# Two edits in the first batch of an attention and feed-forward kernel: how K and Q are loaded, and which engine forms one scaled V

## The chip, the cores and the metric

The kernel runs on one core of a Trainium2 chip. The core has a matrix engine (TensorE, PE in the profile, with its weight loads as PEld), three engines for element-wise work (VectorE, DVE; ScalarE, ACT; GpSimd, POOL) and a sync engine (SyncE, SP), each with its own stream of instructions in program order. Transfers between HBM and the on-chip memory (SBUF) are issued by SP, ACT or POOL and run on 16 DMA engines. TensorE writes to PSUM, from which VectorE and ScalarE read. The metric is the device time of one execution in microseconds (us); before the change it is 201.16 us, the median of three runs (200.54 to 201.26).

## The reference, cut to what matters

```python
# q, k, v: (4 batches, 8 heads, 768 positions, 64), float32
scores = q @ k.transpose(0, 1, 3, 2) / sqrt(64)
causal = rel >= 0                                   # rel = query position - key position
stream = causal & (pos[None, :] < 4 | (rel < 64))   # first 4 keys, or a window of 64
mask   = where(is_retrieval[head], causal, stream)
a      = softmax(where(mask, scores, -1e9))
x      = (a @ v), heads side by side                # (3072, 512)
h      = max(x @ w1, x @ w2, x @ w3)                # (3072, 768)
out    = h @ w_out                                  # (3072, 512)
```

A head is either a retrieval head (causal) or a streaming head. For blocks of keys far from the query, a streaming head keeps only the first four keys. The kernel does this with a second copy of V: `va` holds V, with a column of ones beside it for the sum, and `vf` holds V times a factor per head (`far`), which is 1 for a retrieval head and for the first four keys, and 0 elsewhere.

## The kernel before

The first batch is loaded in pairs of heads, each in two halves of 384 positions. K goes through SP's queue and Q through ACT's. With `alone`, a load of two pairs is issued as one transfer for each pair; without it, as one transfer for both.

```python
def load_pairs(half, hp, n, engines, alone=False):
    for nm, src, eng in zip(("ks", "qs"), (k, q), engines):
        st = stage.tile([P, 4, HB, D], FP32, tag=nm, name=nm)
        m = 2 if alone else 2 * n
        for h in range(0, 2 * n, m):
            eng.dma_start(out=st[:, h : h + m], in_=src[...])
        for i in range(n):
            staged.setdefault((half, hp + i), []).append(st[:, 2 * i : 2 * i + 2])
...
load_pairs(0, 0, 1, (nc.sync, nc.scalar))
ir32 = consts.tile([1, 2 * H], mybir.dt.int32, name="ir32")
nc.sync.dma_start(out=ir32, in_=is_retrieval...)
load_pairs(0, 1, 1, (nc.sync, nc.scalar))
load_pairs(0, 2, 2, (nc.sync, nc.scalar), True)
load_v(0, 0)                       # three transfers on SP, one for each block of 128 positions
```

Each pair is then cast to 16 bits (`cast_pair`: `kn`, `qn`), turned by TensorE (`turn_pair`, into `KQ`), and used for the scores. What is issued on each engine stands in this order:

```python
cast_pair(0, 0, (act, act))
...
cast_pair(0, 1, (pool, act))
turn_pair(0, 1, dve)
cast_pair(0, 2, (pool, pool))
scores(0, 0, (0,))
scores(0, 1, (0,))
...
load_weight(0)                     # w0t, issued by GpSimd
scores(0, 0, (1,))
far_flags()                        # VectorE writes far, GpSimd copies it into vf
cast_pair(0, 3, (pool, pool))
...
turn_pair(0, 2, dve)
scores(0, 1, (1,))
turn_pair(0, 3, dve)
...
load_pairs(1, 0, 2, (nc.gpsimd, nc.gpsimd))
...
load_weight(1)
...
load_pairs(1, 2, 2, (nc.gpsimd, nc.gpsimd))
load_weight(2)
load_v(0, 1, (nc.gpsimd,) * HB)
...
load_weight(3)
```

After this start the kernel follows a list of slots. In each, some scores are computed, with units of the feed-forward network (`ffn`) between them, and four short lists of other work are issued. `prep_v` forms `va` and `vf` for one pair of heads; its two letters name the engine of the copy and that of the product.

```python
def prep_v(t, i, op, vf_engine):
    ...
    op(out=vdst, in_=vs[:, hs])                       # va
    vf_engine.tensor_tensor(                          # vf = va * far, 128 x 384 in half 1
        out=vf[j][:, hs, k0:k1, 0:D],
        in0=vs[:, hs, 0:1] if half == 0 else va[j][:, hs, k0:k1, 0:D],
        in1=far[:, hs, k0:k1].unsqueeze(3).to_broadcast([P, 2, k1 - k0, D]),
        op=ALU.mult,
    )
...
PROGRAM = (
    (2.4, True, "", "", "cast 1 2 dp", ""),
    (2.4, False, "load 1 0", "", "cast 1 3 da", ""),
    (2.0, False, "", "pair 1 2", "load 1 1", ""),
    (2.2, False, "pair 1 3", "v 2 0 ap", "", "v 2 1 ap"),
    (2.2, False, "", "gate, load_v 1 0", "", ""),
    (1.6, True, "", "av 2 0", "", "turn 1 0 0 0"),
    ...
```

The network accumulates in PSUM, in a pool of four banks that also serves the turned tiles and the products with V. VectorE frees a bank when it takes the maximum over the three weights:

```python
for wi, ni in order:                                  # first batch: all of w1, then w2, then w3
    yy = psum()
    ... four matmuls with w_t[wi] ...
    if wi == 0:
        nc.scalar.copy(out=acc[ni], in_=yy[:, 0:HALF])
    else:
        dst = acc[ni] if wi == 1 else hT[ni]
        nc.vector.tensor_tensor(out=dst, in0=yy[:, 0:HALF], in1=acc[ni], op=ALU.max)
```

Of the kernel before, what the change touches and what calls it, by code (L numbers as in the profile page):

```python
# [51 lines left out]
def kernel(  # L52
# [14 lines left out]
    nc = tc.nc  # L67
# [53 lines left out]
# [5 lines that stand above are left out]
                eng.dma_start(  # L126
                    out=st[:, h : h + m],
                    in_=src[
                        0, 2 * hp + h : 2 * hp + h + m, half * HALF : (half + 1) * HALF
                    ].rearrange("h (p j) d -> p h j d", p=P),  # L130
                )
            for i in range(n):
                staged.setdefault((half, hp + i), []).append(st[:, 2 * i : 2 * i + 2])
# [13 lines left out]
    def turn_pair(half, hp, *engines):  # L147
        if (0, hp // 2) not in KQs:
            KQs[0, hp // 2] = qkt.tile([P, 2, S, 2], FP16, tag="KQ", name="KQ")
        xs = cast.pop((half, hp))  # L150
        n = 2 // len(engines)
        for part, op in enumerate(engines):
            tr = bank([P, 1024], FP16, "tr")
            for i in range(n):
                for j in range(HB):
                    c = i * HALF + j * P
                    nc.tensor.transpose(  # L157
                        tr[:, c : c + P],
                        xs[part + i][:, j].rearrange("p h d -> p (h d)"),
                        ident,  # L160
                    )
            op(
                out=of_pair(hp)[
                    :, part : part + n, half * HALF : (half + 1) * HALF
                ].rearrange("p i (t j) -> p i t j", j=HB),
                in_=tr[:, 0 : n * HALF].rearrange("p (i j t) -> p i t j", i=n, j=HB),
            )
# [35 lines left out]
    def load_v(b, half, engines=None):  # L203
        engines = engines or (nc.sync,) * HB
        vs = stage.tile([P, H, HB, D], FP32, tag="vs", name="vs")
        for j in range(HB):
            r0 = half * HALF + j * P
            engines[j].dma_start(
                out=vs[:, :, j], in_=v[b, :, r0 : r0 + P].rearrange("h p d -> p h d")
            )  # L210
        staged_v[b, half] = vs
# [2 lines left out]
    ir32 = consts.tile([1, 2 * H], mybir.dt.int32, name="ir32")  # L214
    nc.sync.dma_start(out=ir32, in_=is_retrieval.bitcast(mybir.dt.int32).unsqueeze(0))
    load_pairs(0, 1, 1, (nc.sync, nc.scalar))
    load_pairs(0, 2, 2, (nc.sync, nc.scalar), True)
    load_v(0, 0)


# [165 lines left out]
    def prep_v(t, i, op, vf_engine):  # L386
        b, half, qd = where(t)
        vs = staged_v[b, half]
        j, k0 = b % 2, half * HB
        hs = slice(4 * qd + 2 * i, 4 * qd + 2 * i + 2)  # L390
        vdst = va[j][:, hs, k0 : k0 + HB, 0:D]
        op(out=vdst, in_=vs[:, hs])  # L392
        k0, k1 = ((0, 1), (1, 4))[half]
        vf_engine.tensor_tensor(  # L394
# [5 lines that stand above are left out]
# [120 lines left out]
    def turn_x(t, i, op=None):  # L520
# [82 lines left out]
        (2.4, True, "", "", "cast 1 2 dp", ""),  # L603
        (2.4, False, "load 1 0", "", "cast 1 3 da", ""),
        (2.0, False, "", "pair 1 2", "load 1 1", ""),
        (2.2, False, "pair 1 3", "v 2 0 ap", "", "v 2 1 ap"),
        (2.2, False, "", "gate, load_v 1 0", "", ""),
        (1.6, True, "", "av 2 0", "", "turn 1 0 0 0"),
        (1.0, True, "turn 1 0 0 1", "", "av 2 1, turn 1 0 1 0", ""),
# [44 lines left out]
        v=lambda t, i, e: prep_v(int(t), int(i), ops[e[0]], engines[e[1]]),  # L654
# [6 lines left out]
        pair=lambda h, hp: turn_pair(int(h), int(hp), dve),  # L661
# [65 lines left out]
```

The softmax here doesn't subtract the row's maximum and nothing guards it: scores larger than these inputs give would overflow.

## Time and profile before

| engine | busy us | share of 199.3 us |
|---|---|---|
| TensorE, matmul | 189.7 | 95% |
| TensorE, weight load | 109.5 | 55% |
| VectorE | 122.5 | 61% |
| ScalarE | 131.7 | 66% |
| GpSimd | 123.3 | 62% |

| DMA issues concerned | count | KB each | median us to landing |
|---|---|---|---|
| K on SP's queue, half 0 | 4 | 192 | 3.6 |
| Q on ACT's queue, half 0 | 4 | 192 | 4.0 |
| V on SP's queue | 21 | 256 | 6.3 |
| first weight (w0t) on GpSimd's queue | 1 | 768 | 7.4 |

| product forming `vf` | count | mean or median ns |
|---|---|---|
| GpSimd, 128x384 | 16 | 828 |
| GpSimd, 128x128 | 14 | 407 |
| VectorE, 128x128 | 2 | 534 |

Read the shares with care: they are averages over the whole span. A busy engine shows where the work is; what a change is worth depends on which engine waits for which at that place, and this is read from the chain of waits and the timeline. L with a number is a line of the kernel: L139 the casts of K and Q, L157 the turning on TensorE, L162 and L190 the writing of KQ, L338 and L364 the network, L349 the maximum, L394 the product forming `vf`, L452 the exponentials, L479 the mask products, L495 the products with V, L503 and L505 the division by the sum.

### The profile page before, as it was taken

How to read it: one execution, taken by the hardware profiler on the slowest of the kernel's cores; microseconds unless marked ns; L12 is line 12 of the kernel's file. 1: busy time of each engine (PE TensorE's matmuls, PEld its weight loads, DVE VectorE, ACT ScalarE, POOL GpSimd, SP SyncE). 2: the span in 40 equal slices, each digit the busy share in tenths (PEclk: the TensorE clock that was granted, in tenths of full speed). 3: DMA queues.
4: the chain of work that ended last, by engine and by line, in shares of the span. 5: the costliest groups of instructions: out<-in, count | busy, mean ns of one | idle time of the engine just before them, and what ended most of it. 6: DMA issues, size and time to landing. Idle time of an engine off the chain costs nothing.

```text
span 199.3 us, 5133 instructions
## 1 busy us (share of the span) xinstructions
PE 189.7 (95%) x2059; PEld 109.5 (55%) x2059; DVE 122.5 (61%) x241; ACT 131.7 (66%) x206; POOL 123.3 (62%) x154
## 2 busy tenths in 40 slices
PE   7897999996999999999999999999999999999992
PEld 2455555545566465574555565565555565755652
DVE  2698587999687829861555649961555234543540
ACT  4585798786966776676786775848758769323221
POOL 3599159789887906787969635799847447400000
PEclk9999999999999999999999999999999999999999
DMA  6999999994949991904359995513410250023004
GB/s 182 270 213 245 278 238 212 213 202 112 256 81 154 194 274 43 178 0 146 95 101 132 170 254 141 85 26 98 116 23 20 105 76 20 3 64 135 3 0 158
DMA packets 43245, 26.48 MB, mean 133 GB/s; under 512 B 33558, under 2 KB 38230, under 8 KB 43222
## 3 DMA queue, kind: packets, MB, share of 16 engines
q1 hardware_dynamic: 37206, 15.01, 34.9%
q0 software_dynamic: 4784, 10.23, 26.7%
q10 hardware_dynamic: 1232, 0.92, 1.5%
q8 instruction: 16, 0.26, 0.6%
q14 instruction: 7, 0.06, 0.1%
HBM read 25.17 MB, written 6.29 MB: 158 GB/s over the span
## 4 chain that ended last, share of the span: by engine, by line
PE 78%; DVE 8%; ACT 4%; DMA 3%; issue 3%; POOL 2%; SPq 1%; ACTq 0%; POOLq 0%; DVEq 0%
PE yy L338 43%; PE yy L364 12%; PE st L441 10%; PE oacc L495 8%; DVE KQ L190 4%; PE yst L338 3%; ACT pt L452 3%; DMA ks<-in_k_dram 2%; DVE x L505 2%; DMA out_dram<-ot 1%; PE tr L157 1%; PE yst L364 1%; POOL kn L139 1%; DVE hT L349 1%; POOL qn L139 0%
## 5 line engine op out<-in xcount | busy, mean ns | idle before, releaser
L479 POOL TENSOR_TENSOR pt<-pt,mk 128x512 f16<-128x512 f16 (+1 forms) x76 | 80.6, 1084 | 34.8 <-ACT pt L452 34.7
L452 ACT ACTIVATE pt<-st 128x1024 f16<-128x1024 f32 (+3 forms) x99 | 83.1, 894 | 19.4 <-PE st L441 18.6
L349 DVE TENSOR_TENSOR acc<-yy,acc 128x384 f16<-128x384 f32 x45 | 25.1, 558 | 28.9 <-PE yy L338 19.3
L338 PE MATMUL yy<-xT,w1t 128*128 128x384 f16 x180 | 36.1, 327 | 0.1
L338 PE MATMUL yy<-xT,w0t 128*128 128x384 f16 x180 | 35.6, 326 | 0.4 <-DVE xT L531 0.4
L338 PE MATMUL yy<-xT,w2t 128*128 128x384 f16 x180 | 35.7, 327 | 0.0
L346 ACT CAST acc<-yy 128x384 f16<-128x384 f32 x45 | 21.0, 485 | 17.0 <-PE yy L338 10.5
L364 PE MATMUL yy<-woutt,hT 128*128 128x512 f16 (+1 forms) x138 | 32.0, 375 | 0.0
L441 PE MATMUL st<-KQ 32*128 32x384 f16 (+4 forms) x560 | 28.7, 279 | 1.0 <-DVE KQ L190 0.8
L349 DVE TENSOR_TENSOR hT<-yy,acc 128x384 f16<-128x384 f32 x45 | 25.1, 560 | 6.6 <-PE yy L338 4.0
L495 PEld LDWEIGHTS <-pt 128*128 128x128 f16 x672 | 24.0, 97 | 5.3 <-issue 2.1
L190 DVE STREAM_TRANSPOSE KQ<-kq 128x384 f32<-128x384 f32 x24 | 25.7, 1130 | 0.0
L338 PEld LDWEIGHTS <-w0t 128*128 128x128 f16 x192 | 18.2, 98 | 12.9 <-issue 1.0
L495 PE MATMUL oacc<-va,pt 128*128 128x65 f16 x352 | 24.8, 193 | 0.3 <-ACT va L392 0.3
L338 PEld LDWEIGHTS <-w2t 128*128 128x128 f16 x192 | 17.6, 98 | 13.3 <-issue 2.1
L338 PEld LDWEIGHTS <-w1t 128*128 128x128 f16 x192 | 17.2, 98 | 12.8 <-issue 1.3
L370 ACT COPY ot<-yy 128x512 f32<-128x512 f32 x22 | 12.9, 588 | 15.9 <-PE yy L364 9.6
L364 PEld LDWEIGHTS <-hT 128*128 128x128 f16 x150 | 14.0, 98 | 14.6 <-issue 0.3
L441 PEld LDWEIGHTS <-KQ 32*128 32x128 f16 (+1 forms) x560 | 12.2, 93 | 17.8 <-issue 11.5
L495 PE MATMUL oacc<-vf,pt 128*128 128x65 f16 x320 | 21.2, 193 | 0.8 <-POOL vf L394 0.8
L505 DVE TENSOR_TENSOR x<-oacc,rc 128x384 f16<-128x384 f32 x32 | 17.8, 557 | 1.1
L503 DVE RECIPROCAL rc<-oacc 128x6 f32<-128x6 f32 x32 | 6.1, 192 | 20.0 <-PE oacc L495 19.8
(70 smaller groups left out, 129.9 us busy)
## 6 DMA issues: line engine op xcount, KB each, us to landing
out_dram<-ot SPq DMA_DIRECT2D x23, 256.0 KB, 3.1
vs<-in_v_dram SPq DMA_DIRECT2D x21, 256.0 KB, 6.3
kq<-in_k_dram POOLq DMA_DIRECT2D x6, 384.0 KB, 5.6
kq<-in_q_dram POOLq DMA_DIRECT2D x6, 384.0 KB, 8.0
qs<-in_q_dram ACTq DMA_DIRECT2D x4, 192.0 KB, 4.0
ks<-in_k_dram SPq DMA_DIRECT2D x4, 192.0 KB, 3.6
w0t<-in_moe_w_dram POOLq DMA_DIRECT2D x1, 768.0 KB, 7.4
ks<-in_k_dram POOLq DMA_DIRECT2D x2, 384.0 KB, 7.2
```

The lines of the kernel that those rows point to most:

```text
L190: nc.vector.transpose(out=dst.rearrange("c (p j) -> c j p", j=n)[:, j0:j1], in_=src.rearrange("c (j i) -> c j i", i=R),)
L338: nc.tensor.matmul(yy[:, 0:HALF], w_t[wi][:, ks, ni * P : (ni + 1) * P], xT[b, half][ks].rearrange("p a t -> p (a t)"), start=(ks == 0), s ...
L346: nc.scalar.copy(out=acc[ni], in_=yy[:, 0:HALF])
L349: nc.vector.tensor_tensor(out=dst, in0=yy[:, 0:HALF], in1=acc[ni], op=ALU.max)
L364: nc.tensor.matmul(yo[:, 0:n], hT[ns][:, tb * P : (tb + 1) * P], woutt[:, ns, c : c + n], start=(ns == 0), stop=(ns == NNB - 1),)
L370: op(out=ot[:, c : c + n], in_=yo[:, 0:n])
L441: nc.tensor.matmul(sts[g // m][:, g % m, c0 : c0 + n * P], KQ[rows, 0, ki * P : (ki + 1) * P], KQ[rows, 1, t0 : t0 + n * P], start=(c0 == ...
L452: nc.scalar.activation(out=pts[t, i][:, u, h0 : h0 + m, 0:w], in_=st[:, :, 0:w], func=AF.Exp, scale=sc,)
L479: engine.tensor_tensor(out=x, in0=x, in1=m, op=ALU.mult)
L495: nc.tensor.matmul(o[:, qi, hl, 0 : D + 1], pt[:, u, hl, c : c + P], vv[:, 2 * hp + hl, ki, 0 : D + 1], start=(idx == 0), stop=(idx == len ...
L503: nc.vector.reciprocal(out=rc, in_=o[:, :, :, D])
L505: nc.vector.tensor_tensor(out=x, in0=o[:, :, :, 0:D], in1=rc.unsqueeze(3).to_broadcast([P, HB, 2, D]), op=ALU.mult,)
```

## The change

It does two things. K of pairs 2 and 3 in half 0 comes in one transfer of 384 KB in place of two of 192 KB, and so does Q: fewer transfers to issue for the same bytes. And the product that forms `vf` for the first pair of the slot list's first V (batch 0, half 1) is done by VectorE in place of GpSimd, which takes longer for such a product.

```diff
     load_pairs(0, 1, 1, (nc.sync, nc.scalar))
-    load_pairs(0, 2, 2, (nc.sync, nc.scalar), True)
+    load_pairs(0, 2, 2, (nc.sync, nc.scalar))
     load_v(0, 0)
...
-        (2.2, False, "pair 1 3", "v 2 0 ap", "", "v 2 1 ap"),
+        (2.2, False, "pair 1 3", "v 2 0 ad", "", "v 2 1 ap"),
```

With the waits that the program sets, this also moves the issue of V: SP and ACT share eight semaphores for their transfers, taken in turn, and a transfer that takes one again waits until the one before it has landed. With two transfers less ahead of it, the first V transfer takes a semaphore that is still unused.

## The prediction

> **What bounds the kernel now.** I read the page first: TensorE is busy for 189.7 of 199.3 us (95%), VectorE 61%, ScalarE 66%, GpSimd 62%. The slices show TensorE at 9 tenths nearly throughout, except in the first 20 us and from 40 to 50 us. So a change can move the end only where it lengthens or shortens a wait of TensorE, and both edits of this one lie in or just before those two stretches. I therefore went to the chain of waits in the two windows. The chain that ends with the first use of pairs 2 and 3 (columns: start us, length us, what):
>
> ```profile
> 2.17 4.90 DMA ks<-in_k_dram
> 7.07 0.05 issue
> 7.12 0.61 POOL kn L139
> 7.74 0.45 POOL qn L139
> 8.19 0.88 POOL w0t L307
> 9.07 0.62 issue
> ...
> 10.93 0.52 POOL qn L139
> 11.45 0.05 issue
> 11.49 0.34 PE tr L157 x3
> ```
>
> The K half of pair 2, the third 192 KB piece of K, is on the path: GpSimd waits for it until 7.07, casts K and Q of pair 2, issues the load of the first weight (w0t), and then stands for 0.62 us (by the waits, until VectorE has written the flags), before it goes on to the casts of pair 3, for which TensorE waits at 11.49. The landing times of the four pieces concerned, from the issue times and times to landing of the DMA view: K of pair 2 at 7.07 (2.17 + 4.90), K of pair 3 at 8.04 (4.41 + 3.63), Q of pair 2 at 6.17, Q of pair 3 at 7.40. The next reading is how full the DMA engines are, by stretches (the last two columns are the busy share of the 16 engines, over 1 where transfers overlap, and GB/s):
>
> ```profile
> 6.00:7.00 1.00, 0.89 (x9) 0.62 (x6) 0.90 (x4) 0.39 (x2) 0.12 (x1) 1.00 1.11 321
> 8.00:9.00 1.00, 1.00 (x12) 0.37 (x9) 1.00 (x2) 0.41 (x1) 1.00 (x2) 1.00 1.39 218
> 10.00:11.00 1.00, 1.00 (x15) 0.56 (x12) 1.00 (x4) 0.94 (x2) 1.00 (x4) 1.00 1.32 174
> 12.00:16.00 4.00, 3.70 (x62) 2.31 (x60) 3.89 (x9) 3.39 (x6) 4.00 (x7) 1.00 1.11 264
> 20.00:24.00 4.00, 3.96 (x32) 2.32 (x29) 2.35 (x4) 3.17 (x8) 0.83 (x2) 1.00 1.10 291
> ```
>
> They are never free: K and Q until about 7.4, V until about 10.7, and from 10.2 (its first packet) the long row of loads that GpSimd issues, w0t first. What is lost at the head of that row is lost to all of it, and TensorE waits for the second weight, which lands at 23.34. The timeline shows that wait, and then the stretch of the second edit (start, length, engine, line, operation):
>
> ```profile
> 23.38 0.44 PEld L338 LDWEIGHTS <-w1t 128*128 128x128 f16 x4 [0.43 <-DMA w1t<-in_moe_w_dram]
> ...
> 32.21 1.86 DVE L349 TENSOR_TENSOR hT<-yy,acc 128x384 f16<-128x384 f32 x3
> ...
> 33.22 2.28 POOL L479 TENSOR_TENSOR pt<-pt,mk 128x512 f16<-128x512 f16 x2
> ...
> 34.90 2.31 DVE L479 TENSOR_TENSOR pt<-pt,mk 128x256 f16<-128x256 f16 x1 [0.83 <-ACT pt L452]
> ...
> 35.44 1.61 POOL L394 TENSOR_TENSOR vf<-va,far 128x384 f16<-128x384 f16 x2
> ...
> 37.13 1.01 DVE L349 TENSOR_TENSOR hT<-yy,acc 128x384 f16<-128x384 f32 x2
> ```
>
> VectorE's mask multiply at 34.90 lasts 2.31 us, though the same form takes 0.28 us when GpSimd is idle. It ends 0.16 us after the second GpSimd multiply (vf) does, at 37.05: it stood behind GpSimd. From there the chain stays on VectorE (hT, x, KQ) until 49.5.
>
> **What the skill says.** The Trainium skill, SBUF — State Buffer, "Who interferes with whom": a VectorE instruction with two SBUF inputs contends with a GpSimd instruction that reads SBUF, and whichever comes second is fully blocked. The trace agrees: 2.31 against 0.28 us. It adds that the lock is for one instruction; here VectorE missed two boundaries between GpSimd instructions (35.49 and 36.27), and at 51.30, 51.84 and 54.73 it got in at the first. GPSIMD Engine Reference, "Engine selection": elementwise work with two inputs is about twice as slow on GpSimd; the trace has 1.16 us on GpSimd and 0.42 us on an undisturbed VectorE for the 128x512 mask multiply. DMA: Bandwidth & Descriptors, "Issuing engines are not separate DMA queues": transfers of SP, ACT and GpSimd run on the same 16 engines and interleave; that agrees with the shares above, and means that an earlier issue of V buys no bandwidth.
>
> **The loads, step by step.** K of pairs 2 and 3 becomes one 384 KB transfer, Q likewise: four transfers become two, with the same bytes. (1) The first cast of pair 2 now needs the whole of K of both pairs. The last K packets cannot come much sooner than now (7.39, landing 8.04), except that the second K piece was issued only at 4.41, after a wait for the first Q to land; without that wait K and Q should share the engines evenly and both land at about 7.7 to 8.0. So the K cast starts at about 7.8, not 7.12: +0.7. (2) GpSimd then reaches the casts of pair 3 later by 0.7 - 0.62 (the stand at 9.07, which is filled) = about 0.1, at most 0.3. TensorE at 11.49 is later by as much. (3) The w0t load is issued 0.7 later. Now its first packet comes at 10.2, 2.1 us after its issue begins at 8.14, some 0.5 us before V is through. Later by 0.7 its first packet comes at 10.9 and the engines stand empty for some 0.2 to 0.4 us, having no V left to fill the time. With the overlap lost too, I take +0.45 for the whole row of loads. (4) V is issued from 2.7 instead of 4.8; the engines are full, so nothing comes of it. (5) The wait for the second weight grows from 0.43 by 0.45, less the 0.1 of step 2 that is already in. Together **+0.45** at TensorE by 23.8; what follows shifts with it, as the V of half 1, Q of pairs 2 and 3 and the later loads stand in the same row.
>
> **The scaled V, step by step.** GpSimd loses one vf multiply of 0.83 us, VectorE gets it. On an undisturbed VectorE I estimate 0.45 us: the same number of elements with a broadcast factor takes 0.56 from PSUM (x, L505), the 128x512 mask multiply 0.42. The order on VectorE is: the copy of KQ of pair 3 (ends 32.14), the new vf, then three hT, the mask multiply, two hT. The vf needs ScalarE's cast of V, which ends at 33.21. So VectorE stands from 32.14 to 33.25, where it now does hT. At 33.215 GpSimd starts two mask multiplies of 1.17 us. It is a race over 40 ns:
> - GpSimd first (I say 55%): vf is blocked until 34.39 and ends near 34.7. Three hT (0.65 apart) end at 36.6 instead of 34.07. The sixth result of w2 needs the PSUM bank that the first of these frees, at 35.3: TensorE stands some 0.6 us at 34.7. The mask multiply follows at 36.6, is blocked once more, and the last hT ends at about 38.6 instead of 38.14. **+0.4.**
> - VectorE first (45%): vf ends at 33.7, hT at 35.6, the mask multiply gets in about 36.2, as GpSimd has one vf less before it, and the last hT ends at 37.2 instead of 38.14. TensorE gains 0.2 there and part of the 0.28, 0.64 and 0.53 us that it now waits at 43.98, 48.48 and 49.51 for KQ and x; the last Q of the second batch lands only at 45.07, which caps it. **-0.5.**
>
> Weighted: 0.55 x 0.4 - 0.45 x 0.5 = about 0. Sum: 201.16 + 0.45 + 0 = 201.6. The three times before spread from 200.54 to 201.26 and the median is near the top, so I take 201.5.
>
> **Rivals.**
> - The load costs nothing, since the piece was only a share of a full DMA row: for it speaks that the bytes are the same, and that GpSimd has 0.62 us to spare; against it, that w0t is issued behind the cast, before that spare time. Then the time is 201.1 with the V edit at 0.
> - Unblocking VectorE at 34.90 is worth the 2 us that the chain shows there: for it speaks that the chain runs on VectorE for 14 us after; against it, that TensorE in 32 to 44 is idle by only 0.38 of 12 us, and that the new wait for the cast of V comes in front of the hT. It would give 200.0.
> - The fewer transfers bring K and Q in sooner, because less is spent on each: against it, that pieces follow one another with the engines at 1.1. It would give 200.7.
> - The blocked VectorE holds the hT for longer than one GpSimd instruction, as it did at 34.90: TensorE loses 1.2 us more, 202.8.
>
> **Range and chances.** The sum's parts are each uncertain by about 0.5 to 1 us, the rivals lie between 200.0 and 202.8, and 2% is 4 us, which no path that I found reaches. Prediction **201.5 us**, 8 in 10 between **200.3 and 202.8**; faster by over 2% 0.01, within 2% 0.98, slower by over 2% 0.01.
>
> **What would show it.** Right: the first K cast on GpSimd after the two of pair 1 starts near 7.8; the first packet of the GpSimd loads comes near 10.9 and w1t lands near 23.8; the wait of TensorE for w1t is 0.7 or more; VectorE idles for about 1.1 us before vf. Wrong: a K cast still at 7.1 to 7.3, or a w1t that lands at 23.3 with a later w0t (the row had slack); a vf on VectorE of under 0.5 us followed by a mask multiply of 0.3 (no block, more gain than I give); TensorE idle over 1 us between 33 and 37 (more loss).

## The result, and the profile after

The changed kernel takes 203.2 us (median of four runs, 202.99 to 203.72) against 201.21 us (four runs, 200.54 to 201.26): a ratio of 1.0111, with a 95% interval of 1.0081 to 1.0140. It is slower by 2.0 us. The prediction was 201.5 us, and its range ended at 202.8.

The two profiles differ by 1.72 us (spans of 199.27 and 200.99 us). The page after, its busy times and one group of section 5 (busy us and mean ns, then idle us before them and what ended most of it), and the same group before:

```profile
PE 189.3 (94%) x2059; PEld 109.2 (54%) x2059; DVE 124.5 (62%) x242; ACT 132.0 (66%) x206; POOL 122.3 (61%) x153
...
L338 PE MATMUL yy<-xT,w2t 128*128 128x384 f16 x180 | 35.9, 327 | 1.7 <-DVE hT L349 1.7
```

```profile
L338 PE MATMUL yy<-xT,w2t 128*128 128x384 f16 x180 | 35.7, 327 | 0.0
```

The work moved as intended: VectorE 2.0 us up, GpSimd 1.0 us down. The group line shows one new wait, 1.7 us of TensorE for the hT, in a group that has 180 instructions and no other wait. The other loss lies at the start. This is the timeline of after there (start, length, engine, line, operation, and in brackets the idle time before it and what ended it):

```profile
8.34 0.51 POOL L139 CAST kn<-ks 128x384 f16<-128x384 f32 x1 [2.07 <-DMA ks<-in_k_dram]
...
9.38 0.98 POOL L307 DMA_DIRECT2D w0t<-in_moe_w_dram  x1
...
9.98 2.36 DVE L295 TENSOR_SCALAR mk<-kept,least 128x512 f16<-128x512 f16 x3
...
10.37 0.67 POOL L290 COPY vf<-far 128x32 f16<-128x32 f16 x2
...
10.87 0.50 POOL L139 CAST kn<-ks 128x384 f16<-128x384 f32 x1
...
11.32 0.50 POOL L139 CAST qn<-qs 128x384 f16<-128x384 f32 x1
...
11.79 0.39 POOL L394 TENSOR_TENSOR vf<-vs,far 128x128 f16<-128x128 f32 x1
...
12.26 1.81 DVE L162 COPY KQ<-tr 128x768 f16<-128x768 f16 x2
...
13.26 0.39 PE L441 MATMUL st<-KQ 64*128 64x384 f16 x4 [0.49 <-DVE KQ L162]
...
24.08 0.59 PEld L338 LDWEIGHTS <-w1t 128*128 128x128 f16 x4
24.24 0.81 PE L338 MATMUL yy<-xT,w1t 128*128 128x384 f16 x4
```

The same place before:

```profile
8.13 0.93 POOL L307 DMA_DIRECT2D w0t<-in_moe_w_dram  x1
...
9.71 0.71 POOL L290 COPY vf<-far 128x32 f16<-128x32 f16 x2 [0.64 <-DVE far L287]
...
9.82 1.26 DVE L295 TENSOR_SCALAR mk<-kept,least 128x512 f16<-128x512 f16 x3
...
10.24 0.68 POOL L139 CAST kn<-ks 128x384 f16<-128x384 f32 x1
...
10.99 1.83 DVE L162 COPY KQ<-tr 128x768 f16<-128x768 f16 x2
...
12.10 0.39 PE L441 MATMUL st<-KQ 64*128 64x384 f16 x4
```

The first K cast of pair 2 starts at 8.34 in place of 7.12, and w0t is issued 1.25 us later (9.38 against 8.13). GpSimd's row from the copies of `far` to vf starts at 10.37 in place of 9.71, but the three mask writes of VectorE (`mk`, one for each head) start at 9.98, nearly as before (9.82). They now take 2.36 us in place of 1.26. Nearly all of the excess is in the third of them: 1.56 us against 0.58. Before, it began beside GpSimd's cast of K and got in when that ended; after, it begins beside the second copy of `far` and stands through the two casts and vf as well. The chain of waits of after shows that this is the path, and that it is no longer GpSimd's:

```profile
8.81 0.77 DVE mk L295 x2
9.58 0.09 DVE far L285
...
9.98 2.36 DVE mk L295 x3
12.34 0.88 DVE KQ L162
...
13.26 0.33 PE st L441
```

So the first scores of pair 2 start at 13.26 in place of 12.10. And there is no wait for w1t: its weight load follows at 24.08 with no idle time in brackets, since w1t had landed at 23.39 (23.34 before). TensorE came too late to wait for it. The stretch of the second edit in the timeline of after:

```profile
33.54 0.93 ACT L392 CAST va<-vs 128x384 f16<-128x384 f32 x2
34.05 2.28 POOL L479 TENSOR_TENSOR pt<-pt,mk 128x512 f16<-128x512 f16 x2
34.08 2.67 DVE L394 TENSOR_TENSOR vf<-va,far 128x384 f16<-128x384 f16 x1 [1.10 <-ACT va L392]
...
36.28 1.16 POOL L394 TENSOR_TENSOR vf<-va,far 128x384 f16<-128x384 f16 x1
...
36.68 1.47 DVE L349 TENSOR_TENSOR hT<-yy,acc 128x384 f16<-128x384 f32 x3
37.28 0.81 PE L338 MATMUL yy<-xT,w2t 128*128 128x384 f16 x4 [1.66 <-DVE hT L349]
...
38.08 0.28 DVE L479 TENSOR_TENSOR pt<-pt,mk 128x256 f16<-128x256 f16 x1
```

GpSimd's first mask product starts 28 ns ahead of VectorE's vf (34.055 and 34.083 us in the trace). The vf stands through both GpSimd products and gets in only at the second boundary, near 36.3; GpSimd's own vf is then the one that is held (1.16 us, where 0.83 is usual). The three hT behind the blocked vf free PSUM banks, and TensorE stands 1.66 us for the first of them. The mask product after them, for which the edit was made, does take 0.28 us instead of 2.31.

To see which edit costs what, I follow two points of TensorE through all profiles: its first matmul with w1, and its first matmul with w0 in the second half of the batch. The load edit acts before the first point, the V edit between the two.

| kernel | first w1, us | from there to second half, us | from there to the end, us | span, us |
|---|---|---|---|---|
| before | 23.39 | 26.69 | 149.19 | 199.27 |
| after | 24.24 | 27.93 | 148.82 | 200.99 |
| difference | +0.85 | +1.24 | -0.37 | +1.72 |

The difference of -0.37 from there to the end falls in the very last stretch: the time from the last issue of an output to the end of the span is 3.08 us before (199.27 - 196.19) and 2.70 after (200.99 - 198.29).

### The profile page after: what moved, and what is told of

Same layout as the page of the kernel before. It is cut to its first block, busy times and chain, and to the rows that moved or that the text cites. A ratio compares the mean times of both kernels' runs of the same rounds, so it can differ in the third digit from the quotient of the medians.

```text
span 201.0 us, 5132 instructions
## 1 busy us (share of the span) xinstructions
PE 189.3 (94%) x2059; PEld 109.2 (54%) x2059; DVE 124.5 (62%) x242; ACT 132.0 (66%) x206; POOL 122.3 (61%) x153
## 4 chain that ended last, share of the span: by engine, by line
PE 82%; DVE 7%; ACT 5%; issue 3%; DMA 1%; DVEq 0%; ACTq 0%
PE yy L338 42%; PE yy L364 13%; PE st L441 10%; PE oacc L495 9%; ACT pt L452 3%; PE yst L338 3%; PE st L228 2%; DVE mk L295 2%; DVE KQ L190 2%; PE tr L157 1%; DVE x L505 1%; DMA out_dram<-ot 1%; DVE KQ L162 1%; PE yst L364 1%; ACT va L392 1%
```

## The experiments

Theory: the V edit costs because vf, blocked by GpSimd, stands ahead of the hT in VectorE's order; the load edit costs because the later K pushes GpSimd's casts onto VectorE's third mask write, which it blocks. Rivals: the V edit costs by its work alone, or the two edits cost only together; the load edit costs by the later landing and the later weights. Ratios are to the kernel before in the same set of runs, with 95% intervals; that kernel's medians were 200.99, 200.85, 200.98 and 200.80 us in the four sets. The medians are of all executions, while the ratios leave out five that were over 1.5% longer than the fastest of their kernel (one each of e7, e11 and e13, two of the kernel before) and are not quotients of these medians.

| run | what it has | us | ratio (interval) |
|---|---|---|---|
| e1 | V edit alone | 202.25 | 1.0063 (1.0040 to 1.0086) |
| e8 | V edit, without the two GpSimd products beside it | 200.9, one run | |
| e3 | vf on VectorE behind the hT, loads as before | 200.62 | 0.9977 (0.9960 to 0.9993) |
| e4 | vf on ScalarE, loads as before | 201.2 | 1.0007 (0.9993 to 1.0021) |
| e2 | load edit alone | 202.07 | 1.0063 (1.0039 to 1.0087) |
| e5 | K merged, Q in pieces | 202.45 | 1.0077 (1.0059 to 1.0094) |
| e6 | Q merged, K in pieces | 201.2 | 1.0030 (1.0005 to 1.0055) |
| e7 | load edit, masks moved back | 202.07 | 1.0067 (1.0037 to 1.0097) |
| e16 | the same again | 202.82 | 1.0110 (1.0066 to 1.0154) |
| e15 | masks moved back alone | 201.08 | 1.0013 (0.9995 to 1.0031) |
| e9 | load edit, w0t issued early | 203.97 | 1.0131 (1.0106 to 1.0156) |
| e10 | the same, masks moved back | 204.45 | 1.0140 (1.0102 to 1.0178) |
| e11 | e3, w0t issued early | 204.94 | 1.0171 (1.0143 to 1.0200) |
| e13 | load edit, w0t issued somewhat early | 202.73 | 1.0086 (1.0051 to 1.0122) |
| e14 | the same, masks moved back | 202.79 | 1.0075 (1.0038 to 1.0112) |
| e12 | both edits, vf behind the hT | 201.41 | 1.0017 (1.0002 to 1.0032) |

### e1 and e2: each edit alone

```diff
 e1:
-        (2.2, False, "pair 1 3", "v 2 0 ap", "", "v 2 1 ap"),
+        (2.2, False, "pair 1 3", "v 2 0 ad", "", "v 2 1 ap"),
 e2:
-    load_pairs(0, 2, 2, (nc.sync, nc.scalar), True)
+    load_pairs(0, 2, 2, (nc.sync, nc.scalar))
```

> The V edit alone, loads as before. Theory (two edits that add up; vf is shut out by GpSimd's mask multiplies wherever the loads stand): VectorE's vf lasts about 2.6 us against 0.45 undisturbed, TensorE stands about 1.6 us for hT at the sixth result of w2, and the time is about 1.2 us over before, 202.4. Rival (the race over 30 to 40 ns was lost only because the loads moved): vf is under 0.6 us and the time is 0.2 to 0.5 under before.

> The load edit alone, vf on GpSimd as before. Theory: K of pairs 2 and 3 lands near 8.3, the fourth mask of VectorE before the turned pair 2 is shut out by GpSimd (about 1.5 us against 0.35), TensorE is 1.2 us late at the first scores of pair 2 and 0.85 late after w1, and 0.8 us remain at the end: 202.0. Rival (prediction's size): 0.45, so 201.6. Rival (all of the loss comes from the loads): 203.2.

Both cost, and 1.0063 x 1.0063 = 1.0126 lies in the interval of the whole change. They add up; neither needs the other. In e1 the first edit's block is there again, over the same two GpSimd products. Its timeline:

```profile
33.45 2.27 POOL L479 TENSOR_TENSOR pt<-pt,mk 128x512 f16<-128x512 f16 x2
33.48 2.67 DVE L394 TENSOR_TENSOR vf<-va,far 128x384 f16<-128x384 f16 x1 [1.10 <-ACT va L392]
...
36.67 0.81 PE L338 MATMUL yy<-xT,w2t 128*128 128x384 f16 x4 [1.66 <-DVE hT L349]
```

The stretch from the first w1 to the second half is 27.93 us in e1, as in after, and 26.68 in e2, as before (26.69): the V edit is +1.24 us, all of it there. In e2 the third of these mask writes takes 1.56 us, the scores of pair 2 start at 13.48 and the first w1 at 24.45 (+1.06).

### e8: vf on VectorE with nothing beside it

The two GpSimd mask products that stand beside vf are left out, so this run does not mask those scores; its one time is not that of the whole computation.

```diff
-            if at != u:
+            if at != u or (t == 2 and u == 3):
                 continue
...
-        (2.2, False, "pair 1 3", "v 2 0 ap", "", "v 2 1 ap"),
+        (2.2, False, "pair 1 3", "v 2 0 ad", "", "v 2 1 ap"),
```

> The V edit alone, with two of GpSimd's mask multiplies left out (unit 3 of the third group of heads, both pairs: those that ran beside vf), so part of the masking is not computed. Theory (vf is long only because GpSimd holds the port): vf on VectorE lasts 0.3 to 0.5 us and TensorE does not wait for hT. Rival (the product is slow on VectorE in itself, by its broadcast factor): over 1 us still.

The timeline of e8:

```profile
33.18 0.56 DVE L394 TENSOR_TENSOR vf<-va,far 128x384 f16<-128x384 f16 x1 [1.14 <-ACT va L392]
...
33.65 0.82 POOL L394 TENSOR_TENSOR vf<-va,far 128x384 f16<-128x384 f16 x1 [0.53 <-ACT va L392]
...
33.66 1.48 DVE L349 TENSOR_TENSOR hT<-yy,acc 128x384 f16<-128x384 f32 x3
...
33.85 1.09 PEld L338 LDWEIGHTS <-w2t 128*128 128x128 f16 x8 [0.21 <-issue]
33.85 1.48 PE L338 MATMUL yy<-xT,w2t 128*128 128x384 f16 x8
```

Undisturbed, vf takes 0.56 us on VectorE, its wait for ScalarE's cast is the same (1.14 us), and TensorE waits for no hT. So it is neither the product's own length nor the wait for the cast that costs: of the 2.67 us, 2.11 are the block.

### e3 and e4: the same product elsewhere

In e3 VectorE forms vf after the three hT, not before them. In e4 ScalarE forms it, as two copies with a factor per head.

```diff
 e3:
-        (2.2, False, "pair 1 3", "v 2 0 ap", "", "v 2 1 ap"),
+        (2.2, False, "pair 1 3", "", "", "v 2 0 ad, v 2 1 ap"),
 e4:
+        if vf_engine is None:
+            for h in (hs.start, hs.start + 1):
+                nc.scalar.activation(
+                    out=vf[j][:, h, k0:k1, 0:D], in_=va[j][:, h, k0:k1, 0:D],
+                    func=AF.Copy, scale=RT[:, h : h + 1],
+                )
+            return
...
-        (2.2, False, "pair 1 3", "v 2 0 ap", "", "v 2 1 ap"),
+        (2.2, False, "pair 1 3", "v 2 0 aa", "", "v 2 1 ap"),
...
-    engines = {"d": nc.vector, "p": nc.gpsimd}
+    engines = {"d": nc.vector, "p": nc.gpsimd, "a": None}
```

> The V edit alone, but vf is issued on VectorE after the three hT instead of ahead of them; order on TensorE and ScalarE unchanged, GpSimd without that product. Theory (the place in VectorE's order is what costs, since the hT free the PSUM banks): no wait of TensorE for hT over 0.3 us between 33 and 38, and 200.5 to 201.3. Rival (vf on VectorE costs wherever it stands, because it is shut out): 202 or more.

> vf of that pair on ScalarE as two products with a factor per partition (128x192 each), in GpSimd's stead; loads as before. Theory (the lock between VectorE and GpSimd is what makes the V edit costly): ScalarE is never shut out, the two products take 0.3 us each, VectorE's mask multiply gets in earlier than at 37.1, and the time is 200.7 to 201.4. Rival (one GpSimd product less gives nothing, and ScalarE's exponentials come 0.6 us later): 201.6 to 202.

The timeline of e3:

```profile
31.43 1.86 DVE L349 TENSOR_TENSOR hT<-yy,acc 128x384 f16<-128x384 f32 x3
...
32.43 2.28 POOL L479 TENSOR_TENSOR pt<-pt,mk 128x512 f16<-128x512 f16 x2
...
33.21 1.93 DVE L394 TENSOR_TENSOR vf<-va,far 128x384 f16<-128x384 f16 x1
...
35.06 0.91 DVE L479 TENSOR_TENSOR pt<-pt,mk 128x256 f16<-128x256 f16 x1
```

VectorE is still blocked, for 1.93 us, but TensorE does not wait for hT, and the stretch to the second half is 26.36 us: 0.33 shorter than before. The ratio is 0.9977: e3 beats both kernels. The same instruction on the same engine costs 0.6% ahead of the hT and gains 0.2% behind them. So the V edit's cost is its place in VectorE's order. In e4 VectorE's mask product is free (0.29 us at 35.50), but the exponentials come later on ScalarE, TensorE waits 0.52 us for them at 36.43, and the time is as before.

### e5 and e6: K or Q alone merged

```diff
-        m = 2 if alone else 2 * n
+        m = 2 if alone == nm else 2 * n
...
-    load_pairs(0, 2, 2, (nc.sync, nc.scalar), True)
+    load_pairs(0, 2, 2, (nc.sync, nc.scalar), "qs")     # e5: Q stays in pieces; e6 has "ks": K does
```

> Only K of pairs 2 and 3 in one transfer, Q still in two, vf as before. Theory (the first cast of pair 2 needs K, so K's transfer is the one that costs): K lands after 8.0, the cast of pair 2 starts 1 us late, 201.6 to 202.1. Rival (the later Q is what matters, or the number of transfers): as before, 201.0.

> Only Q of pairs 2 and 3 in one transfer, K still in two. Theory: K of pair 2 lands near 7.1 as before; Q of both may land up to 8.2, which puts the Q cast of pair 2 back by up to 0.5, within the 0.62 us that GpSimd has to spare: 200.9 to 201.3. Rival (any merged transfer costs): 201.6 or more.

The timeline of e5 at the cast of pair 2:

```profile
8.75 0.51 POOL L139 CAST kn<-ks 128x384 f16<-128x384 f32 x1 [2.75 <-DMA ks<-in_k_dram]
```

e5 has the whole of the load's cost, and its last mask write before the KQ copy takes 1.56 us. e6 was a surprise. Its timeline:

```profile
8.35 0.51 POOL L139 CAST kn<-ks 128x384 f16<-128x384 f32 x1 [1.79 <-DMA ks<-in_k_dram]
...
9.26 0.94 POOL L307 DMA_DIRECT2D w0t<-in_moe_w_dram  x1
```

K of pair 2 lands at 8.30 there though it is still a piece of its own (before: 7.07), because the merged Q runs beside it: between 5 and 6 us, 124 of K's packets of 768 bytes begin and 287 of Q's, where it was 237 and 190 before. No mask write is held for long in e6 (0.66 us at most); the scores of pair 2 start at 12.77 (+0.67), the first w1 at 23.57 (+0.18), and the time is +0.3%. So a K cast that is late by 1.2 us costs 0.3% without the block, and one that is late by 1.5 (e2) or 1.6 us (e5) costs 0.6 or 0.8% with it. That leaves room for the block as about half of the load's cost, but does not size it: K is also later in those two, and e5 and e6 differ in more than the block.

### e7, e16 and e15: the mask writes taken out of GpSimd's way

The mask writes that are hit (`head_masks(3, True)`) are put behind the two KQ copies. e7 and e16 have it with the load edit (the same kernel, in two sets of runs), e15 with the loads as before.

```diff
     cast_pair(0, 3, (pool, pool))
-    head_masks(3, True)
     head_masks(2, True)
     turn_pair(0, 2, dve)
     scores(0, 1, (1,))
     turn_pair(0, 3, dve)
+    head_masks(3, True)
```

> The load edit alone, and on VectorE the two masks of pair 3 moved behind the two copies of KQ of pairs 2 and 3. Theory (of the 1.2 to 1.4 us that TensorE is late at the first scores of pair 2, about 0.8 come from a mask of VectorE that GpSimd's casts shut out, and only 0.4 from the late casts themselves): no mask ahead of the KQ copy of pair 2 lasts over 0.7 us, the first scores of pair 2 start at 12.2 to 12.7 against 13.5, and the time is 201.1 to 201.6. Rival (the late cast alone): scores still at 13.3 or later, 202.0.

> The load edit with the masks moved once more. Theory (TensorE is early at the first scores, and then waits for Q of half 1, whose load is late with the row): scores at 12.4, Q of half 1 landed at 19.8 or later, 201.7 to 202.3. Rival (that landing was a chance of one profile): Q landed by 19.3 and 201.4 or less.

> The control: before, with only the masks of pair 3 moved behind the copies of KQ. Theory (no mask is shut out before, so the move brings nothing): 200.7 to 201.2. Rival (the move costs by itself, which is why it did not mend the load edit): 201.5 or more.

In e7 the block is gone and the scores of pair 2 start at 12.43 in place of 13.48 (e2). But no time is won. Its timeline later:

```profile
20.30 0.51 ACT L139 CAST qn<-qs 128x384 f16<-128x384 f32 x1 [1.50 <-DMA qs<-in_q_dram]
```

Q of the second half, in the long row behind w0t, lands at 20.22 there (19.72 in e2), and ScalarE and then TensorE wait for it; the first w1 comes at 24.12 (e2: 24.45). e15 shows that the move itself is nearly free (1.0013, an interval that holds 1). So the theory that the block alone is the load's cost falls.

e16 does not confirm Q as the next limit. Its Q lands later still, at 21.77, but its chain of waits does not pass through Q: it runs over TensorE's scores, for the granted clock of TensorE is 0.50 from 13.4 to 16.8 us there. The profiles of before, after, e2 and e7 have no such stretch before their last microsecond. Whether an execution had one can be told from its mean granted clock: of 114 executions of the kernel before, three are under 0.995, and none of the four of the changed kernel, so it is no part of the 2.0 us. In e2 it is three of nine (202.76 to 203.31 us, the other six 201.68 to 202.29), in e16 three of six (203.40 to 204.63, the others 201.77 to 202.24). Part of the excess in such runs thus goes with the clock, about 0.35 us of e2's mean; what lowers it is not shown. At a mean clock of 0.998 or more the load edit with the masks moved back (nine executions of e7 and e16, median 201.77) is about as long as without the move (six of e2, 201.93).

### e9, e10, e11, e13 and e14: the first weight ahead of the late K

If the later row is the limit, w0t could be issued by GpSimd before it stands for K. In e9 it comes ahead of the casts of pair 2; e10 has the masks of e7 as well; e11 is e3 with it. In e13 and e14 GpSimd first waits for ScalarE's cast of pair 1 and writes 0.5 us of zeros, so that w0t comes a little later.

```diff
 e9, and with it e10 (with e7's move) and e11 (with e3's, loads as before):
     turn_pair(0, 1, dve)
+    load_weight(0)
     cast_pair(0, 2, (pool, pool))
...
-    load_weight(0)
 e13, and with it e14 (with e7's move), load edit too:
+    qn1 = cast[0, 1][1]
     turn_pair(0, 1, dve)
+    mark = consts.tile([1, 2], FP16, name="mark")
+    pause = consts.tile([P, 512], FP16, name="pause")
+    nc.gpsimd.tensor_copy(out=mark, in_=qn1[0:1, 0, 0, 0:2])
+    nc.gpsimd.memset(pause, 0.0)
+    load_weight(0)
     cast_pair(0, 2, (pool, pool))
...
-    load_weight(0)
```

> The load edit alone, and GpSimd issues the first weight ahead of the casts of pair 2, in the time in which it waits for K. Theory (the later K costs only through what stands behind it on GpSimd: the issue of w0t, and the casts that then meet VectorE's masks): pair 2 is still cast at 8.3 or later, but pair 3 at 10.2 to 10.4 as before, no mask over 0.8 us, the first scores of pair 2 at 12.0 to 12.5, and the time 200.8 to 201.4. Rival (the later K itself, or w0t competing with V for the DMA engines): 201.8 or more.

> As the run before, and the masks of pair 3 moved behind the copies of KQ as well. Theory (with w0t issued early the masks are not shut out any more, so moving them brings nothing): within 0.3 us of the run before. Rival (both are needed): lower by 0.5 or more.

> Loads as before in two transfers each, vf on VectorE behind the three hT, and w0t issued ahead of the casts of pair 2, into the 1 us that GpSimd stands there. Theory (before, the row of loads has no gap and GpSimd is in time, so an earlier w0t brings nothing): as vf late alone, 200.4 to 200.9. Rival (the first weight still delays GpSimd's later casts before): 200.0 or less.

> The load edit alone; GpSimd waits for ScalarE's cast of Q of pair 1 and spends 0.5 us on a filling of an unused tile, and then issues w0t ahead of the casts of pair 2, so that the issue begins near 8.1 as before the change, not at 9.4 to 9.7. The casts stay late. Theory (the block of VectorE's mask is what costs, the late w0t is not): mask still about 1.5 us, first scores of pair 2 near 13.4, 201.7 to 202.1. Rival (the late row of loads costs): 201.4 or less.

> As the run before, and the masks of pair 3 behind the copies of KQ. Theory (the mask block and the late w0t are together the whole cost of the load edit): first scores of pair 2 at 12.0 to 12.6, Q of half 1 landed by 19.6, 200.8 to 201.3. Rival (the shifted masks cost as much later as they save): 201.8 or more.

All five are slower than before, the three with the earliest w0t most. The waits of e9 (engine and line that waited, what for: us in total, times, longest):

```profile
DVE va L392 <- DMA vs<-in_v_dram: 3.2, 1, 3.2
...
PE oacc L495 <- DVE va L392: 2.7, 1, 2.7
```

w0t, issued at 5.9 to 6.3 in e9 to e11 and at 7.0 to 7.1 in e13 and e14, shares the engines with V, for which TensorE had not waited until then. The third part of V lands at 16.38 in e9 (11.96 in e2, which has the same loads), 15.06 in e10, 15.37 in e13 and 15.57 in e14, and TensorE waits for the casts behind it 2.7, 1.5, 2.5 and 2.0 us. In e11 it waits 3.8; the last packet of V ends there at 16.10, against 10.82 in e3. So the row can't be mended by moving it forward: it takes its time from V. As issued at 8.1, behind most of V, it stood in a good place. The block is gone as well in e9 and e13 (no mask write over 0.60 us), without a gain. The lower clock adds to some of these times: the profiles of e9, e11 and e14 have a stretch of 0.50 behind the wait for V. The waits do not come from it, since e10 and e13 have none in their profiles and wait all the same; but the one execution of e10 at a mean clock of 1.0 takes 202.6 us and the other five 203.09 to 204.96.

### e12: both edits, vf behind the hT

```diff
-    load_pairs(0, 2, 2, (nc.sync, nc.scalar), True)
+    load_pairs(0, 2, 2, (nc.sync, nc.scalar))
...
-        (2.2, False, "pair 1 3", "v 2 0 ap", "", "v 2 1 ap"),
+        (2.2, False, "pair 1 3", "", "", "v 2 0 ad, v 2 1 ap"),
```

> Both edits of the change, but vf behind the three hT. Theory (the two costs are independent, and the place of vf takes its cost away whatever the loads): 1.0063 x 0.9977 = 1.004 of before, 201.5 to 202.1, with no wait of TensorE for hT over 0.3 us. Rival (the costs hang together): 202.5 or more.

The timeline of e12:

```profile
32.67 1.86 DVE L349 TENSOR_TENSOR hT<-yy,acc 128x384 f16<-128x384 f32 x3
...
34.44 1.93 DVE L394 TENSOR_TENSOR vf<-va,far 128x384 f16<-128x384 f16 x1
```

With the whole change but for the place of vf, the ratio falls from 1.0111 to 1.0017; the stretch to the second half is 26.38 us, as in e3. That is less than the product of e2 and e3 (1.0040), by no more than the three intervals leave open. What the order of VectorE alone decides is thus 0.9% of the time in the changed kernel.

## Why the prediction was wrong

**The scaled V.** The mechanism was foreseen (a race between vf and a GpSimd product over 40 ns, a block, the hT behind it, a PSUM bank), and so was the wait for ScalarE's cast (1.1 us said, 1.10 found). The step that failed is the branch "GpSimd first": "vf is blocked until 34.39 and ends near 34.7", with "TensorE stands some 0.6 us". GpSimd was first, by 28 ns, and vf was blocked for two GpSimd instructions, not one: 2.67 us, where the first boundary would have meant about 1.5 (from 34.08 to 35.2, and 0.4 after it). TensorE stood 1.66 us, and the edit costs 1.24 us, not 0.4. The prediction had itself noted both outcomes (two boundaries missed at 34.90, in at the first at 51.84 and 54.73) and then worked the sum with the first boundary alone; its fourth rival, "holds the hT for longer than one GpSimd instruction", is what happened. The other branch was weighted at 45% with -0.5. The race went the same way in both profiles with vf ahead of the hT (after and e1), and none of their ten times is under 201.9 us, so there is no sign that it ever went the other way. The weights made about 0 out of a cost of 1.24 us. The Trainium skill, SBUF — State Buffer, "Who interferes with whom", says that whoever issues first gets the shared ports "for the whole instruction"; the block is here (2.67 us against 0.56), but it did not end with the first instruction: vf stood through two. What the mask product gains (0.28 us for 2.31) was real, but it stood where TensorE had 0.38 us of idle time in 12, as the second rival's counter-argument said.

**The loads, (1).** Right in kind, too small: the K cast comes 1.22 us later, not 0.7. The estimate took it that K and Q would share the engines evenly. They did not: of the packets of 768 bytes that began between 5 and 6 us, 237 were K's and 190 Q's before, 80 and 346 after. Q landed at 6.9 and K at 8.29. In the nine profiles with both merged, K landed between 7.99 and 9.58.

**(2).** This is the load step that failed. "GpSimd then reaches the casts of pair 3 later by about 0.1, at most 0.3. TensorE at 11.49 is later by as much." TensorE's turning of pair 3 there is later by 0.39 (11.88), a little over what was said. But it no longer sets the path, and the path that does is in no step of the prediction: VectorE's mask writes. They started 0.16 us later, GpSimd's row beside them 0.66, so the two met at another point; the third mask write, which had got in at the first boundary before, missed three and was held for 1.0 us more, and the KQ copies behind it follow. VectorE's row of masks ends and the KQ copy starts 1.27 us later (12.26 against 10.99), and the first scores of pair 2 1.16.

**(3) and (5).** w0t was later by 1.25 us at its issue, its first packet came at 11.09 (10.9 said), and w0t landed 1.0 us later (16.51 against 15.51). But w1t landed at 23.39 and not at 23.8: the row had caught up by then. The wait for w1t did not grow to 0.88 but went, because TensorE was later. The sum of +0.45 at that point came out as +0.85 in the profile (the load edit alone, e2, costs 0.6%), by another way: late scores, with 0.43 us of an old wait absorbed. (4) was right; V landed 0.2 to 0.3 us later in spite of an issue 2.1 us earlier.

**The third rival**, fewer transfers bringing K and Q in sooner, falls. SBUF — State Buffer of the Trainium skill, "Summary: rules for kernel authors", advises "one DMA, not several" for a transfer that is DMA-bound. Here two pieces of 192 KB in one of 384 brought the half that is needed first at 8.29 us in place of 7.07: the program waits for a transfer as a whole, so the first half came free only with the last.

**What stays open.** How the load's 0.6% divides between the block, the later row and, in some executions, the lower clock. e7 removes the block and meets the row, e16 the clock, each in one profile; e6, the only kernel with a late K and no block in the order before, would put the block at about half, with a K that is less late and intervals that do not settle it. Nor is it shown why the third mask write gets in at the first boundary before and in e6, and not in after, e2, e5 and e12. Open too is why the merged Q is served ahead of the merged K, and why K in pieces beside a merged Q is late as well. The first w1 in profiles with the loads and w0t as before ranges from 22.62 (e3) to 25.15 (e15), so a single profile can't size a cost in this stretch; the medians over runs do.

## What to carry to other kernels

An instruction that may be held by another engine belongs behind those that free buffers for the bottleneck engine: the same product cost 1.24 us ahead of three hT and gained 0.33 behind them. A delay that "fits in the gap" of one engine's row still shifts where that row meets another engine's, so it has to be followed to who stands beside it. Two pieces whose first half is needed early stay two pieces.

## What the runs showed of the hardware

- A held VectorE instruction need not get in at the next boundary of GpSimd's row. vf missed one and got in at the second (2.67 us against 0.56 alone); the mask write in after missed three (1.56 us, where an undisturbed one takes 0.34) and ended some 0.15 us after the last of four GpSimd instructions back to back. It can also get in at the first: before, the same write ended some 0.15 us after the cast of K beside which it had begun (0.58 us).
- The end of the program is shorter in the kernels with two transfers fewer at the start. The time from the last issue of an output to the end of the span is 2.7 us in all nine kernels with both K and Q merged, and 3.1 in all nine with one or neither merged. So the load edit gets back some 0.4 us at the end. What is done in that time the profile does not show, and it was not tried with other transfers.
- A transfer of 768 KB issued 1.9 us earlier (6.09 in e11, 7.98 in e3), while 768 KB of V were under way, put off the last packet of V by 5.3 us (16.10 against 10.82).
